# A two-stage attention and highway kernel: a fixed instruction order, a finer softmax chain, and part of the k norms taken off the matrix engine

## The chip, the cores and the metric

The kernel runs on one core of one Trainium2 chip. A core has five engines, each with its own in-order queue: TensorE (PE, with its weight loads shown as PEld), VectorE (DVE), ScalarE (ACT), GpSimd (POOL) and SyncE (SP, here used only to issue transfers). They meet through semaphores. The metric is the device time of one execution in microseconds. Before the change it was 270.34 us, the median of three runs (270.19 to 270.39). The profiled execution spans 268.3 us from its first to its last instruction; the difference of 2.0 us lies outside the span.

## What is computed

Four batches of q, k and v, each 6336 x 256 in float32, are turned into an attention over channels (a 256 x 256 matrix for each batch), and its result goes through a highway layer.

```python
qn = q / (np.linalg.norm(q, axis=1, keepdims=True) + 1e-06)     # norm over the 6336 rows
kn = k / (np.linalg.norm(k, axis=1, keepdims=True) + 1e-06)
s  = kn.transpose(0, 2, 1) @ qn / tau                           # 256 x 256 for each batch
a  = softmax(s, axis=-1)
x  = (v @ a).reshape(4 * 6336, 256)
H  = np.maximum(x @ w_h, 0.0)
T  = 1.0 / (1.0 + np.exp(-(x @ w_t + b_t)))
out = T * H + (1.0 - T) * x                                     # float32, 25344 x 256
```

The three inputs are 77.9 MB to read and the output is 26 MB to write.

## The kernel before

A batch has 50 row blocks s: 48 of 128 rows in 6 chunks of 8 (j = 0 to 5), and two of 96 rows (j = 6). Loads are issued by GpSimd and convert float32 to float16 on the way; stores and the four transposing transfers are issued by SyncE.

**Stage 1** of a batch multiplies k by q on TensorE for all 50 blocks, into two PSUM tiles. Beside the product itself it needs the sums of squares of each column of q and k. They are the diagonals of two more products, k by k and q by q:

```python
def stage1(b, s):                        # 50 of these for each batch
    for c in range(2):
        nc.tensor.matmul(sg[c][:, 0:C], kc, qa, ...)                  # 256 columns: the product
        nc.tensor.matmul(sg[c][:, C : C + P], kc, kc, ...)            # 128 columns: squares of k
        if not apart(b, s // CH):                                     # apart: b > 0 and j < 5
            nc.tensor.matmul(sg[c][:, C + P : C + 2 * P], qa[:, cs], qa[:, cs], ...)   # squares of q
```

For batches 1 to 3 the squares of the first five q chunks are made elsewhere: ScalarE squares half a chunk at a time (128 x 1024), GpSimd adds the halves and folds them, and one small matmul with a column of ones (`sumps`) sums over the partitions.

```python
nc.scalar.activation(out=sq, in_=qa, func=Act.Square)      # 30 of them
add(out=sq, in0=sq, in1=other)                             # GpSimd, 128x1024
add(out=sq[:, 0:2, :], in0=sq[:, 0:2, :], in1=sq[:, 2:4, :])      # 128x512
add(out=sq[:, 0, :], ...); add(out=sums[b], ...)           # 128x256 each
```

**The chain** between the stages turns the sums into softmax weights: `diagonal` reads the diagonals, `norm` is a power of 0.5 on GpSimd, `recip` and `dcat` make a diagonal matrix of the inverse norms, `bcast` spreads it with a matmul against ones, `scale` and `exp` make the softmax numerators, `trans` and `fold` multiply them by the two weight matrices, and `soft` and `evac_ah` write the three parts of the tiles `mr0` and `mr1`, which every matmul of stage 2 reads.

**Stage 2** of a batch takes 25 pairs of blocks; g counts them over all batches (0 to 99). For each pair: `tr` transposes v on TensorE and `ev` copies it out of PSUM (in the last batch chunks 3 to 6 are transposed by a transfer instead, four such transfers in all); `h`, `t` and `x` are four matmuls of 256 columns each; `b` sets the bias in PSUM by a copy; `r` (ReLU) and `g` (tanh) run on ScalarE; `p` and `y` on VectorE. A store takes four pairs.

```python
products(h, b, i, 1, ...)                       # h: 4 matmuls 128x256 on TensorE, line 800
copy(e, t[0:nr], bias_all[0:nr])                # b: ScalarE or VectorE
products(t, b, i, 2, ...)                       # t
nc.scalar.activation(out=d, in_=h, func=Act.Relu, scale=0.5)          # r
products(d, b, i, 0, ...)                       # x, added to d
nc.scalar.activation(out=uu, in_=t, func=Act.Tanh, scale=-0.5)        # g
nc.vector.scalar_tensor_tensor(out=pp, in0=uu, scalar=1.0, in1=d, ...)   # p
nc.vector.scalar_tensor_tensor(out=ot, in0=h, scalar=0.0, in1=pp, ...)   # y
```

The order of all of this on the engines is found while the program is built: each task has a key, and a small list scheduler (`Plan.run`, with the table of keys `PRIO`) picks what stands next. Loads stop between the end of stage 1 and the second norm (`loads_stop`). The tile buffers are 5 chunks for each of q, k and v and 7 for the output. Early stores are held back by small transfers (`hold`) that make SyncE wait for a later output chunk.

Of the kernel before, what the change touches and what calls it, by code (L numbers as in the profile page):

```python
# [15 lines left out]
P = 128  # L16
# [6 lines left out]
AHEAD = 16  # L23
BY_DMA = 3
SHORT = 1.08
MOVE = 165e3
APART = 5
V_AHEAD = 2


PRIO = {
    "tr": (24.974, 16.445, 34.195, 63.304),
    "ev": (74.59, 73.008, 67.512, 50.704),
    "h": (-53.39, -86.015, -64.208, -14.641),
    "bias": (-28.394, 23.065, -1.772, 4.453),
    "t": (4.111, -1.918, 67.766, 74.312),
    "relu": (46.555, -20.175, -1.498, 14.915),
    "x": (0.958, -19.433, 43.343, -6.4),
    "gate": (-54.132, 37.28, -94.231, -112.222),
    "prod": (-40.861, -10.819, -26.763, -55.482),  # L40
    "res": (53.604, 18.42, 116.457, -9.113),
    "s1": (117.419, 42.459, 84.45),
    "sq": (-15.195, 72.384, 19.395),
}
POW = 0.75
HEAD = 5.5
TAIL = 66
EV = BIAS = ("ACT", "DVE")
ENDS = [18, 48.5, 62.25]


class Ring:


    def __init__(self, bufs):
        self.bufs = bufs
        self.freed = []

    def open_at(self, t):
        n = len(self.freed) - self.bufs  # L60
        return n < 0 or (self.freed[n] is not None and self.freed[n] <= t)


class Task:
# [3 lines left out]

    def __init__(self, eng, key, pitch, lat, deps, fn, take=(), drop=(), size=0, follows=()):
        self.eng, self.key, self.pitch, self.lat = eng, key, pitch, lat
        self.deps, self.fn, self.take, self.drop, self.size = deps, fn, take, drop, size
        self.follows = follows
        self.start = self.done = None
        self.late = 0.0
        self.soft = 0
        self.held = {}
        self.serial = False

    def engines(self):
        return self.eng if isinstance(self.eng, tuple) else (self.eng,)

    def settle(self, e):
        n = self.eng.index(e)
        self.pitch, self.lat = self.pitch[n], self.lat[n]
        self.fn = partial(self.fn, e)
        self.eng = e


class Plan:

# [8 lines left out]
    def __init__(self):  # L101
        self.tasks = []
        self.rings = {}

        self.loads_stop, self.sums_stop = [], []

    def ring(self, tag, bufs):
        self.rings[tag] = Ring(bufs)

    def add(self, *args, **kw):  # L110
        t = Task(*args, **kw)
        self.tasks.append(t)
        return t

    def run(self):
        queues = {"POOL": [], "SP": []}
        in_order = {"POOL": [], "SP": []}
        users, followers = {}, {}
        for n, x in enumerate(self.tasks):
            x.n, x.left, x.at = n, len(x.deps) + len(x.follows), 0.0  # L120
            for d in x.deps:
                users.setdefault(d, []).append(x)
            for d in x.follows:
                followers.setdefault(d, []).append(x)
            if x.size or x.serial:
                in_order[x.eng].append(x)
        for lst in in_order.values():
            lst.sort(key=lambda x: (x.key, x.n), reverse=True)
        engines = list(dict.fromkeys(x.eng for x in self.tasks if not isinstance(x.eng, tuple)))
        avail = {e: [x for x in self.tasks if e in x.engines() and not x.left and not (x.size or x.serial)] for e in engines}  # L130
        free = dict.fromkeys(engines, 2.1)
        lanes, order, events = [], [], [0.0, 2.1]
        t, left = 0.0, len(self.tasks)
        eps = 1e-6

        def ready(x):
            return (
                not x.left
                and x.at <= t + eps
                and all(self.rings[g].open_at(t + eps) for g in x.take)  # L140
                and (x.eng != "POOL" or not x.size or sum(d > t + eps for d in lanes) < self.LANES)
            )

        def finish(x, when):
            x.done = when
            events.append(when)
            for owner, tag in x.drop:
                self.rings[tag].freed[owner.held[tag]] = when
            release(users.get(x, ()), when)

        def release(us, when):
            for u in us:
                u.left -= 1
                u.at = max(u.at, when)
                if not u.left and not (u.size or u.serial):
                    for e in u.engines():
                        avail[e].append(u)

        def pick(e):
            quiet = held(self.sums_stop)  # L160
            best = min(
                (x for x in avail[e] if ready(x) and not (quiet and x.soft >= quiet)),
                key=lambda x: (x.key, x.n), default=None,
            )
            lst = in_order.get(e)
            if best is None and lst and ready(lst[-1]) and not (e == "POOL" and held(self.loads_stop)):
                return lst[-1]
            return best

        def held(stops):  # L170
            return next(
                (
                    n + 1 for n, (a, b) in enumerate(stops)
                    if a.start is not None and (b.done is None or b.done > t + eps)
                ),
                0,
            )

        while left or any(queues.values()):
            for e in engines:  # L180
                x = pick(e) if free[e] <= t + eps else None
                if x is None:
                    continue
                if x.size or x.serial:
                    in_order[e].pop()
                else:
                    for other in x.engines():
                        avail[other].remove(x)
                    if isinstance(x.eng, tuple):
                        x.settle(e)  # L190
                left -= 1
                x.start = t
                order.append(x)
                for g in x.take:
                    x.held[g] = len(self.rings[g].freed)
                    self.rings[g].freed.append(None)
                free[e] = t + x.pitch
                release(followers.get(x, ()), free[e])
                events.append(max(free[e], t + 2 * eps))
                if x.size:  # L200
                    queues[e].append([x, float(x.size), t + self.HEAD])
                    events.append(t + self.HEAD)
                    if e == "POOL":
                        x.lane = len(lanes)
                        lanes.append(1e9)
                else:
                    finish(x, t + x.lat)

            act = [qq for qq in queues.values() if qq and qq[0][2] <= t + eps]
            share = self.RATE / max(1, len(act))  # L210
            nxt = [x for x in events if x > t + eps] + [t + qq[0][1] / share for qq in act]
            assert nxt, "no task can start"
            nxt = min(nxt)
            for qq in act:
                qq[0][1] -= share * (nxt - t)
            t = nxt
            events = [x for x in events if x > t - eps]
            for qq in act:
                if qq[0][1] < 1.0:
                    x = qq.pop(0)[0]  # L220
                    finish(x, t + self.LAG + x.late)
                    if x.eng == "POOL":
                        lanes[x.lane] = t + self.LAG
        self.end = max(x.done for x in order)
        return order
# [3 lines left out]
def kernel(  # L229
# [37 lines left out]
        "sq": 2, "vT": 3, "vT_t": 1, "o": O_BUFS, "ot": 1, "uu": 3, "pp": 3, "vtsb": 9, "mr0": 2, "mr1": 2,  # L267
        "sg0": 1, "sg1": 1, "vt": 1, "t": 1, "h": 2, "d": 2,
# [73 lines left out]
    def plan_load(nm, b, j, s=0, n=CH):  # L342

        size = P * n * C * 4 if j < NJ else TR * 2 * C * 4
        tag = nm if j < NJ else f"tail_{nm}"
        x = plan.add(
            "POOL", len(plan.tasks), 0.54, 0, [], lambda: load(nm, b, j, s, n),
            take=[tag] if s == 0 else [], size=size * (1 if j < NJ and n > 2 else SHORT),
        )
        ld.setdefault((nm, b, j), []).append(x)  # L350
        x.first = s
# [43 lines left out]
    plan_load("v", 0, 0)  # L395


    ends = [(-1, HEAD)] + [(e, (n + 1) * NS) for n, e in enumerate(ENDS)]

    def slot_of(n):  # L400

# [693 lines left out]
```

## Time and profile before

| what | value |
|---|---|
| time, median of 3 | 270.34 us |
| span of the profiled execution | 268.3 us |
| TensorE busy, idle | 246.4 us, 21.9 us |
| VectorE, ScalarE, GpSimd busy | 181.6, 195.1, 131.7 us |
| bytes read from and written to HBM | 78.38 MB, 25.95 MB |
| first matmul starts | 8.95 us |
| last stage-1 matmul of batch 0 starts | 36.69 us |
| first matmul of stage 2 (h of pair 0) | 45.65 us |
| first output store is issued | 101.04 us |
| last matmul starts | 262.04 us |
| last store is issued | 264.60 us |

In the lines of the profile a row names the line of the kernel, the engine, the operation and the tiles it writes and reads, then the number of instructions, the busy time in all and the mean of one in ns. Tables by window give the busy time of each engine in a stretch of the span. "GB/s" counts bytes as they land: a load reads four bytes of float32 from HBM for two bytes of float16 that land, so loads alone at 212 GB/s read 424 GB/s. A store counts once.

### The profile page before, as it was taken

What the parts mean: (1) busy time and instruction counts of PE and PEld (TensorE: products, weight loads), DVE (VectorE), ACT (ScalarE), POOL (GpSimd) and SP (SyncE); (2) the same over time, 40 slices, a digit from 0 to 9 for tenths busy, and PEclk for the clock granted to TensorE, in tenths of its full rate; (3) what the DMA queues carried; (4) which work ended last, traced back from release to release, by engine and by line L of the source; (5) the groups of instructions that cost most, each with busy time, mean ns of one, the idle gap of its engine ahead of it and who ended that gap; (6) DMA issues with size and microseconds to landing.
All of it is one profiled execution on the core that took longest, in us unless ns stands there. A gap on an engine that the chain in (4) does not pass through costs nothing.

```text
span 268.3 us, 6249 instructions
## 1 busy us (share of the span) xinstructions
PE 246.4 (92%) x2430; PEld 216.6 (81%) x2430; DVE 181.6 (68%) x377; ACT 195.1 (73%) x365; POOL 131.7 (49%) x167
## 2 busy tenths in 40 slices
PE   0697977999999999999999999999999999999991
PEld 0596864889989978999999878999998778888880
DVE  1000035777766789557878797586878998998994
ACT  1001016978888789999898887787798999998980
POOL 7233468688778064695689138567655110000000
PEclk9999999999999999999999999999999999999998
DMA  6999999999999999999999999999999999999995
GB/s 107 215 211 208 206 206 202 212 213 214 214 213 212 213 214 255 247 263 269 275 286 258 267 267 254 249 236 281 287 280 239 284 214 304 379 399 165 351 423 232
DMA packets 24622, 67.24 MB, mean 251 GB/s; under 512 B 9104, under 2 KB 11280, under 8 KB 21648
## 3 DMA queue, kind: packets, MB, share of 16 engines
q0 software_dynamic: 13472, 39.20, 75.0%
q1 hardware_dynamic: 11120, 27.64, 29.0%
q8 instruction: 19, 0.31, 0.4%
q14 instruction: 11, 0.09, 0.1%
HBM read 78.38 MB, written 25.95 MB: 389 GB/s over the span
## 4 chain that ended last, share of the span: by engine, by line
PE 76%; DMA 12%; ACT 5%; POOL 2%; issue 2%; DVE 2%; ACTq 0%; DVEq 0%; POOLq 0%
PE h L800 16%; PE t L800 16%; PE d L800 15%; PE sg L452 12%; DMA k<-in_k_dram 10%; PE sg L453 6%; PE vtps L760 5%; DMA v<-in_v_dram 2%; ACT uu L854 2%; PE sg L455 2%; PE t L831 1%; PE vtps L754 1%; PE ah L689 1%; POOL q L327 1%; ACT d L840 1%
## 5 line engine op out<-in xcount | busy, mean ns | idle before, releaser
L800 PEld LDWEIGHTS <-vtsb 128*128 128x128 f16 (+1 forms) x1044 | 98.8, 99 | 17.3 <-issue 3.2
L452 PE MATMUL sg<-q,k 128*128 128x256 f16 x384 | 83.8, 277 | 12.7 <-DMA k<-in_k_dram 12.6
L861 DVE SCALAR_TENSOR_TENSOR pp<-uu,d 128x512 f32<-128x512 f32 (+1 forms) x100 | 68.0, 684 | 28.4 <-PE d L800 16.1
L453 PE MATMUL sg<-k 128*128 128x128 f16 x384 | 76.8, 223 | 0.0
L854 ACT ACTIVATE uu<-t 128x512 f32<-128x512 f32 (+1 forms) x100 | 59.7, 597 | 19.1 <-PE t L800 18.5
L880 DVE SCALAR_TENSOR_TENSOR o<-h,pp 128x512 f32<-128x512 f32 x96 | 65.5, 686 | 1.7
L840 ACT ACTIVATE d<-h 128x512 f32<-128x512 f32 (+1 forms) x100 | 57.9, 584 | 5.7 <-PE h L800 4.9
L800 PE MATMUL t<-mr,vtsb 128*128 128x256 f16 (+1 forms) x348 | 52.2, 272 | 1.5 <-ACT t L533 1.2
L800 PE MATMUL h<-mr,vtsb 128*128 128x256 f16 (+1 forms) x348 | 51.2, 272 | 0.5 <-ACT vtsb L533 0.5
L800 PE MATMUL d<-mr,vtsb 128*128 128x256 f16 (+1 forms) x348 | 51.5, 272 | 0.1
L452 PEld LDWEIGHTS <-k 128*128 128x128 f16 x384 | 38.0, 99 | 16.7 <-DMA k<-in_k_dram 13.9
L476 POOL TENSOR_TENSOR sq<-sq,sq 128x1024 f32<-128x1024 f32 x15 | 35.4, 2361 | 16.7 <-ACT sq L470 16.6
L453 PEld LDWEIGHTS <-k 128*128 128x128 f16 x384 | 38.0, 99 | 1.5
L533 ACT COPY t<-bias_all 128x512 f32<-128x512 f32 (+1 forms) x60 | 35.4, 591 | 1.4
L455 PE MATMUL sg<-q 128*128 128x128 f16 x144 | 32.5, 226 | 0.0
L470 ACT ACTIVATE sq<-q 128x1024 f32<-128x1024 f16 x30 | 31.3, 1053 | 0.0
L760 PE MATMUL vtps<-ident,v 128*128 128x128 f32 x144 | 27.8, 275 | 0.9 <-DMA v<-in_v_dram 0.6
L569 DVE SCALAR_TENSOR_TENSOR junk<-sg,ident 128x128 f32<-128x128 f32 x16 | 4.6, 288 | 33.2 <-PE sg L455 32.7
L535 DVE COPY vtsb<-vtps 128x256 f32<-128x256 f32 (+2 forms) x47 | 19.6, 418 | 7.0 <-PE vtps L760 6.7
L327 POOL DMA_DIRECT2D v<-in_v_dram x24 | 13.7, 571 | 18.9 <-PE vtps L760 11.7
L327 POOL DMA_DIRECT2D q<-in_q_dram x28 | 15.4, 552 | 15.1 <-DMA q<-in_q_dram 7.1
L327 POOL DMA_DIRECT2D k<-in_k_dram x28 | 15.3, 548 | 13.1 <-DMA k<-in_k_dram 9.2
(78 smaller groups left out, 249.5 us busy)
## 6 DMA issues: line engine op xcount, KB each, us to landing
out_dram<-o SPq DMA_DIRECT2D x23, 1024.0 KB, 9.6
v<-in_v_dram POOLq DMA_DIRECT2D x24, 512.0 KB, 16.6
q<-in_q_dram POOLq DMA_DIRECT2D x21, 512.0 KB, 16.2
k<-in_k_dram POOLq DMA_DIRECT2D x21, 512.0 KB, 18.0
q<-in_q_dram POOLq DMA_DIRECT2D x5, 256.0 KB, 9.6
k<-in_k_dram POOLq DMA_DIRECT2D x5, 256.0 KB, 8.9
out_dram<-o SPq DMA_DIRECT2D x2, 512.0 KB, 4.2
out_dram<-ot SPq DMA_DIRECT2D x4, 192.0 KB, 5.1
```

Source lines behind the costliest of these rows:

```text
L327: nc.gpsimd.dma_start(out=t[:, s : s + n, :], in_=main_rows(src)[:, j * CH + s : j * CH + s + n, :])
L452: nc.tensor.matmul(sg[c][:, 0:C], kc, qa, start=first, stop=False)
L453: nc.tensor.matmul(sg[c][:, C : C + P], kc, kc, start=False, stop=False)
L455: nc.tensor.matmul(sg[c][:, C + P : C + 2 * P], qa[:, cs], qa[:, cs], start=False, stop=last)
L476: add(out=sq, in0=sq, in1=other)
L533: nc.scalar.copy(out=out, in_=in_)
L760: nc.tensor.transpose(ps[:, u, 0:nr], v.bitcast(f32), ident0[0:nr, 0:nr])
L800: nc.tensor.matmul(out[0:nr, u, :], vt[u][kt][:, 0:nr], mr[kt][:, col * C : (col + 1) * C], **flags(u, kt))
L840: nc.scalar.activation(out=d[0:nr, :, :], in_=ps_t["h", b, i][0:nr, :, :], func=Act.Relu, scale=0.5)
L854: nc.scalar.activation(out=uu[0:nr, :, :], in_=ps_t.pop(("t", b, i))[0:nr, :, :], func=Act.Tanh, scale=-0.5)
L861: nc.vector.scalar_tensor_tensor(out=pp[0:nr, :, :], in0=el.pop(("uu", b, i))[0:nr, :, :], scalar=1.0, in1=ps_t.pop(("d", b, i))[0:nr, :, ...
L880: nc.vector.scalar_tensor_tensor(out=ot, in0=ps_t.pop(("h", b, i))[0:nr, :, :], scalar=0.0, in1=el.pop(("pp", b, i))[0:nr, :, :], op0=AluO ...
```

## The change

1. **Order.** The scheduler and its keys are gone. Every task has a name, and one string, `ORDER`, lists all 1,528 of them as they are to be recorded, with the engine where there is a choice (`ev0/ACT`).
2. **Norms of k.** For batches 1 to 3, the squares of the first two k chunks leave TensorE, as those of five q chunks did already. The squares are made by ScalarE or VectorE, and a running sum is kept for each batch over all halves, by GpSimd or VectorE, with one fold at the end.
3. **A finer chain.** Diagonals, copies and evictions are separate tasks for each half; the diagonal matrix and the matmul against ones become two matmuls of an inverse norm, broadcast, against the identity; `evac_ah` is split into the part that `h` needs and the part that `t` needs, so that each product waits for its own part alone.
4. Buffers are given back in finer steps (for example `mr0` and `mr1` one by one).

Other forms of stage 2 that the new code can make (`form_b`, `form_d`) are not used: `FORM_B` and `FORM_D` are empty. The four transfers that transpose, the number of stores and loads and all tile sizes are as before.

```diff
-BY_DMA = 3
-APART = 5
-PRIO = { ... }
+BY_DMA = (3, 4, 5, 6)
+OFF = {'q': (0, 5, 5, 5), 'k': (0, 2, 2, 2)}
+ORDER = """
+Lq0.1 Lk0.0 Lq0.0 const Lk0.1 Lk0.2 Lq0.2 Lq0.6 Lk0.6 Lb0 Lb1 Lq0.3 s0.0 s0.1 ...
+... Lw1 s0.40 s0.41 Lv0.0 s0.42 s0.43 Lw0 s0.44 Lq1.0.4 s0.45 s0.46 s0.47 c0.dq1 c0.g0/ACT ball c0.dq0 c0.dk0
+c0.nq sqq1.0.0/ACT c0.dk1 c0.nk c0.iq c0.g1/ACT c0.b Lq1.1 c0.ik s1.0 s1.1 Lk1.1 s1.2 c0.s1 c0.s0 Lv0.1 ...
+"""
@@ stage1
-            nc.tensor.matmul(sg[c][:, C : C + P], kc, kc, start=False, stop=False)
-            if not apart(b, s // CH):
+            if not apart("k", b, s // CH):
+                nc.tensor.matmul(sg[c][:, C : C + P], kc, kc, start=False, stop=False)
+            if not apart("q", b, s // CH):
@@ squares and sums
-        nc.scalar.activation(out=sq, in_=qa, func=Act.Square)
+        if e == "ACT":
+            nc.scalar.activation(out=out, in_=x, func=Act.Square)
+        else:
+            (nc.vector if e == "DVE" else nc.gpsimd).tensor_tensor(out=out, in0=x, in1=x, op=AluOp.mult)
+    def add_square(nm, b, j, n, e):
+        eng, acc = nc.gpsimd if e == "POOL" else nc.vector, acc_t[nm, b]
+        eng.tensor_tensor(out=acc, in0=acc, in1=sq_t.pop((nm, b, j, n)), op=AluOp.add)
@@ chain
-            nc.tensor.matmul(st["cqb"], ones, st["dcat"][:, :, :], start=True, stop=True)
+            for c in range(2):
+                nc.tensor.matmul(
+                    st["cqb"][:, c, :], st["inv"][:, c : c + 1].to_broadcast([P, P]), ident0, ...)
-            o, a, r = mr_t[b][c][:, C : 3 * C], st["ah", c], st["ri"][:, c : c + 1]
+            o = rows_of(c)[:, (n + 1) * C : (n + 2) * C]
+            a, r = st["ah", c][:, n * C : (n + 1) * C], st["ri"][:, c : c + 1]
@@ stage 2
-                "PE", pr("h", g), 0.435, 0.64, [ev] + ready[b] + ends_of[h_bank], ...
+                f"h{g}", "PE", 0.437, 0.64, [ev] + ready[b]["h"] + ends_of[h_bank], ...
```

In `ORDER`, L is a load (Lv0.0 is v, batch 0, chunk 0), s a block of stage 1, c a step of the chain, sqk and adk a square and its addition, O a store, T a transposing transfer and H a hold.

## The prediction

> **What bounds the kernel now.** I read the page's first part, then its slices and queues. TensorE leads by far in busy time, and its slices stand at 9 almost from end to end. But so do those of the transfers:
>
> ```profile
> PE 246.4 (92%) x2430; PEld 216.6 (81%) x2430; DVE 181.6 (68%) x377; ACT 195.1 (73%) x365; POOL 131.7 (49%) x167
> ...
> PE   0697977999999999999999999999999999999991
> ...
> DMA  6999999999999999999999999999999999999995
> GB/s 107 215 211 208 206 206 202 212 213 214 214 213 212 213 214 255 247 263 269 275 286 258 267 267 254 249 236 281 287 280 239 284 214 304 379 399 165 351 423 232
> ...
> q0 software_dynamic: 13472, 39.20, 75.0%
> q1 hardware_dynamic: 11120, 27.64, 29.0%
> ...
> HBM read 78.38 MB, written 25.95 MB: 389 GB/s over the span
> ```
>
> Each slice is 6.7 us. The first 15 hold loads alone (the first store is issued at 101 us), and 212 GB/s landing means 424 GB/s read. Where loads and stores mix, the figure rises because a store counts once; the sum of bytes on the HBM side hardly changes. So the transfers run at one rate, about 424 GB/s, for nearly the whole span. Is TensorE held up by them? The table by window says where it idles, and the list of waits for whom:
>
> ```profile
> 38.00:46.00 8.00, 5.89 (x48) 4.10 (x49) 5.03 (x19) 4.30 (x10) 6.85 (x11) 1.00 1.14 199
> 46.00:100.00 54.00, 53.37 (x526) 47.21 (x524) 39.17 (x80) 46.09 (x84) 36.60 (x44) 1.00 1.07 213
> 100.00:200.00 100.00, 99.07 (x998) 89.54 (x997) 76.41 (x154) 85.82 (x156) 64.19 (x71) 1.00 1.06 264
> 200.00:262.00 62.00, 61.31 (x558) 52.27 (x556) 56.51 (x110) 56.25 (x113) 7.61 (x10) 1.00 1.05 308
> ```
>
> ```profile
> PE sg L452 <- DMA k<-in_k_dram: 12.6, 5, 9.0
> ...
> PE t L800 <- ACT t L533: 1.2, 3, 0.7
> ...
> PE vtps L760 <- DMA v<-in_v_dram: 0.6, 1, 0.6
> ```
>
> The second column after the window is TensorE's busy time. From 46 to 262 us it idles 216.0 - 53.37 - 99.07 - 61.31 = 2.25 us. Before 46 it waits for k, above all 9.0 us for the first chunk, and 2.1 us are idle between 38 and 46, in the chain of batch 0. So TensorE bounds the stretch from 46 on, and its work there is back to back. Yet the transfers have a floor of their own that lies close under the same span. I work it out:
>
> - Start: the first two loads, 2.10 MB read, have landed at 8.95 us when TensorE starts; at 424 GB/s they take 4.95 us, so bytes flow from 4.0 us.
> - Bytes: (78.38 + 25.95) MB / 424 GB/s = 246.1 us.
> - The transposing transfers. The second queue carried 27.64 MB against 25.95 MB stored, so 1.69 MB of transposes: three full chunks and a quarter. The transfer view of 240 to 262 us shows what they cost:
>
> ```profile
> GB/s 387 298 188 61 45 39 142 290 324 247 161 140 45 236 254 188 500 447 268 462 256 358 86 462 462 268 477 477 447 477 268 462 477 462 447 283 477 432 447 417
> ```
>
> Here a slot is 0.55 us. From the second to the sixteenth, 8.25 us, only 2658 x 0.55 = 1.46 MB land; two full transposes (1.04 MB) lie there, and the other 0.42 MB would take 1.0 us. So one costs (8.25 - 1.0) / 2 = 3.6 us, and 3.25 of them 11.8 us. The last 17 slots, stores alone, average 426 GB/s.
> - Sum: 4.0 + 246.1 + 11.8 = 261.9 us, and some 1.5 us (my estimate) from the last byte to the end: **263.4 us** against a span of 268.3. The slack of the transfers is 4.9 us, under 2%.
>
> [...] shares of 75.0% and 29.0% add to over 100% and say nothing, the bytes do. [...] the 684 ns of line 861 at 512 and the 414 ns of line 634 at 256 lead, by their slope of 1.05 ns, to 1.22 us as well. [...]
>
> **The change part by part.**
>
> *Squares of k.* 3 batches x 2 chunks x 8 blocks x 2 halves = 96 matmuls of 128 columns leave TensorE. Their own length in the trace (220 ns) is latency; what counts is the distance to the next start:
>
> ```profile
> 38.33 0.28 PE L452 MATMUL sg<-q,k 128*128 128x256 f16 x1 [1.43 <-DMA k<-in_k_dram]
> 38.45 0.22 PE L453 MATMUL sg<-k 128*128 128x128 f16 x1
> 38.51 0.27 PE L452 MATMUL sg<-q,k 128*128 128x256 f16 x1
> 38.62 0.22 PE L453 MATMUL sg<-k 128*128 128x128 f16 x1
> ```
>
> From 38.45 to 38.51: 0.056 us, so 96 x 0.056 = 5.4 us less. What comes back: three sums over partitions for k, of the kind of line 516, 0.50 us each in the chain view, 1.5 us; and the new broadcast of the inverse norms, four short matmuls for two long ones, some 0.1 us a batch. **Net on TensorE: -3.5 us**, all of it after 38 us, where TensorE is the bound.
>
> *Squares and sums elsewhere.* From the lists of both instruction orders: ScalarE makes 28 squares for 30 (-2 x 1.05), 17 more copies of transposed v (about +6.3), 4 fewer of the wide ones (-2.4), 2 more bias copies (+1.2), and small ones: about +4 us, to 199. VectorE makes 14 squares and 5 sums at 1.22 (+23.2), folds (+1), 17 fewer copies of 0.42 (-7.1) and 4 more of the wide ones (+1.7), 2 fewer bias copies (-1.4), no diagonal matrices (-1.9): about +15 us, to 197. GpSimd makes 31 sums of 2.36 us and 9 us of folds for 74.4 us before: about +8 us, to 140. All three stay near or under three quarters of the span, beside TensorE and not on its path.
>
> *Chain.* In batches 1 to 3 it was nearly hidden: all idle time of TensorE there is within the 2.25 us. In batch 0 the first h starts at 45.65 us after v's first chunk, issued only at 38.88 us. The new order issues that load before block 42 of stage 1, and the parts of the chain overlap more. I put the first pair about 1.5 us earlier. But fewer matmuls of stage 1 are left to fill the gap, as k's squares are gone there, so TensorE gains at most 1.5 us from it.
>
> *Order.* The tasks are mostly where they were: stage 1 of batch 1 ends near pair 18, of batch 2 near pair 43, of batch 3 near pair 64, before and after. I give it nothing of its own. Stage 1 of batch 0 waits for its loads in both.
>
> Sum for TensorE alone: -3.5 - 1.5 = -5.0 us.
>
> **Rivals.** First, *the gain passes through*: 270.3 - 5.0 = 265.3 us. For it speaks that TensorE is without gaps from 46 to 262. Second, *the transfers become the bound*: the bytes and the transposes are unchanged, so at best the span loses 4.9 us, and that only with no gap anywhere. For it speaks that the final stores already run at the full rate from 251 us to the end, behind stores queued at 220 us and transposes; pairs done earlier then only wait in the output buffers. Against it, some of the slack (the dip to 199 GB/s between 38 and 46) goes away with the earlier load of v. I expect 266.5 to 268 us. Third, *VectorE and GpSimd collide*: 19 long operations on VectorE meet GpSimd sums that run a third of the time; waits of up to 2.4 us each in fixed queues could stall TensorE, whose d and h have two PSUM buffers each. That would give 269 to 274 us. The 70 us that VectorE would still be idle speak against it.
>
> **How the number follows.** I take the second as the likeliest: of 5.0 us won on TensorE and 4.9 us of slack in the transfers some 3.1 us come through. 270.3 - 3.1 = **267.2 us**. The range runs from the first rival, 265.3, to a small loss by the third that eats most of the gain, 269.7. Faster by over 2% means under 264.9 us, a span of 262.9, below the floor I worked out: 6%. Slower by over 2% needs stalls of over 8 us net: 4%.
>
> **What would show it.** Right: 288 matmuls of the k-by-k form and TensorE busy time near 243; loads still at 212 GB/s in the first 14 slices; stores at full rate to the end; TensorE with new idle time, or its last matmul earlier by more than the span shrinks, so that the last store ends several us after it. The first h near 44 us. Wrong: a span under 263, which would mean that the transposes cost less beside other traffic than I counted or that the rate can rise; or GpSimd sums well over 2.36 us and VectorE sums well over 1.22 us, with TensorE waiting for d, t or h, which would be the collision.

## The result, and the profile after

The changed kernel takes **307.54 us** (median of four, 306.54 to 308.66) beside 270.26 us for the kernel before: a ratio of 1.138, 95% interval 1.133 to 1.143. It is 37 us slower; 267.2 was predicted, and 269.7 was the upper end of the range.

The page of the changed kernel, the same parts and rows as were shown of before (a slice is now 7.7 us):

```profile
PE 254.4 (83%) x2354; PEld 218.1 (71%) x2354; DVE 209.0 (68%) x383; ACT 200.6 (65%) x385; POOL 140.6 (46%) x150
...
PE   0599877888899999899978896799996999563793
...
DMA  6999999999997999999999999949799999998997
GB/s 122 214 211 207 205 212 214 209 182 198 214 211 138 212 210 201 361 217 199 174 269 212 245 196 276 270 79 405 139 192 352 389 66 104 252 58 193 337 335 285
...
q0 software_dynamic: 13472, 39.20, 69.4%
q1 hardware_dynamic: 11120, 27.64, 31.3%
...
HBM read 78.38 MB, written 25.95 MB: 340 GB/s over the span
```

The bytes are the same to the last digit, and so is most of the work. But the row of 9s is broken: TensorE stands at 5, 6, 3 and 7 near the end, and the transfers fall to 138, 79, 139, 66, 104 and 58 GB/s in single slices; before, only the first slice and one late one (165) lay under 200. Near the end the DMA row stands at 9 in slices where only 66, 104 and 58 GB/s land, so its share does not tell the rate here. The table by window says where TensorE's idle time lies (the second column after the window is its busy time):

```profile
38.00:46.00 8.00, 5.47 (x24) 3.42 (x25) 6.64 (x20) 4.37 (x12) 6.73 (x10) 0.79 1.15 211
46.00:100.00 54.00, 48.04 (x449) 41.23 (x449) 47.75 (x67) 40.90 (x76) 34.81 (x32) 0.97 1.02 195
100.00:200.00 100.00, 89.52 (x808) 77.47 (x806) 79.59 (x153) 79.40 (x153) 66.28 (x60) 0.97 1.03 234
200.00:262.00 62.00, 59.28 (x575) 52.05 (x574) 49.98 (x102) 53.22 (x107) 15.74 (x15) 1.00 0.97 218
262.00:307.00 45.00, 26.55 (x202) 20.96 (x200) 23.70 (x37) 20.65 (x39) 0.53 (x1) 0.84 1.00 241
```

Before, TensorE idled 0.6 us from 46 to 100 and 0.9 from 100 to 200; now 6.0 and 10.5, and some 18 after 262. Between 38 and 46 it runs 24 matmuls where it ran 48. The list of waits of the changed kernel has three that were absent before, or short (engine and line that waited, for what, us in all, times, longest):

```profile
PE h L731 <- DVE o L864: 21.8, 7, 6.6
POOL v L262 <- DMA vT<-v: 21.0, 1, 21.0
DVE o L864 <- DMA out_dram<-o: 20.3, 4, 7.0
```

Read from the bottom: VectorE cannot write a result because its output buffer is still being stored; the next h needs the PSUM buffer that this result would free; and GpSimd cannot issue a load of v because its buffer is still being transposed. A wait for an output buffer was not on the list of before at all, and GpSimd's wait for a transpose was 2.2 us there.

How far the kernel has come is told by the start of the last VectorE operation of a pair (line 880 before, 864 after), in us:

| pair | before | after | e1 | e3 | e9 |
|---|---|---|---|---|---|
| 0 | 48.4 | 51.5 | 52.4 | 49.6 | 48.5 |
| 20 | 99.6 | 108.2 | 107.1 | 103.7 | 100.5 |
| 44 | 159.2 | 173.7 | 169.0 | 169.9 | 160.4 |
| 64 | 205.7 | 226.7 | 216.7 | 223.1 | 208.1 |
| 80 | 236.6 | 258.6 | 245.8 | 254.7 | 239.2 |
| 88 | 248.4 | 286.2 | 258.0 | 277.7 | 250.9 |
| 99 | 263.9 | 302.8 | 273.1 | 294.8 | 266.4 |

The loss grows in steps: 3 us in the first chain, 15 by pair 44, 22 by pair 80, 39 at the end. It has more than one cause.

### The profile page after: what moved, and what is told of

Same layout as the page of the kernel before. It is cut to its first block, busy times and chain, and to the rows that moved or that the text cites. A ratio compares the mean times of both kernels' runs of the same rounds, so it can differ in the third digit from the quotient of the medians.

```text
span 306.7 us, 6113 instructions
## 1 busy us (share of the span) xinstructions
PE 254.4 (83%) x2354; PEld 218.1 (71%) x2354; DVE 209.0 (68%) x383; ACT 200.6 (65%) x385; POOL 140.6 (46%) x150
## 4 chain that ended last, share of the span: by engine, by line
PE 40%; DMA 33%; DVE 15%; issue 4%; SPq 3%; ACT 2%; POOL 2%; DVEq 0%; ACTq 0%; POOLq 0%
DMA out_dram<-o 13%; PE h L731 8%; PE sg L373 8%; PE t L731 8%; PE d L731 7%; DMA v<-in_v_dram 7%; DMA q<-in_q_dram 5%; DMA out_dram<-ot 5%; DVE pp L818 4%; DMA k<-in_k_dram 4%; PE vtps L691 4%; DVE o L864 4%; PE sg L375 3%; SPq L699 2%; DVE sq_k L400 1%
## 5 line engine op out<-in xcount | busy, mean ns | idle before, releaser
L731 PEld LDWEIGHTS <-vtsb 128*128 128x128 f16 (+1 forms) x1044 | 101.6, 100 | 41.3 <-issue 26.6
L373 PE MATMUL sg<-q,k 128*128 128x256 f16 x384 | 81.9, 280 | 12.4 <-DMA q<-in_q_dram 11.4
L404 POOL TENSOR_TENSOR acc_q<-acc_q,sq_q 128x1024 f32<-128x1024 f32 x24 | 57.6, 2401 | 44.7 <-ACT sq_q L398 25.5
L731 PE MATMUL h<-mr,vtsb 128*128 128x256 f16 (+1 forms) x348 | 53.9, 279 | 20.0 <-DVE o L864 15.2
L375 PE MATMUL sg<-k 128*128 128x128 f16 x288 | 60.0, 224 | 0.0
L373 PEld LDWEIGHTS <-k 128*128 128x128 f16 x384 | 38.7, 101 | 13.2 <-DMA k<-in_k_dram 9.9
L375 PEld LDWEIGHTS <-k 128*128 128x128 f16 x288 | 28.7, 100 | 3.7 <-issue 2.4
L482 ACT COPY gs<-sg 128x256 f32<-128x256 f32 x8 | 3.0, 377 | 35.2 <-PE sg L377 35.2
L482 ACT COPY vtsb<-vtps 128x256 f32<-128x256 f32 (+2 forms) x53 | 20.4, 385 | 5.4 <-PE vtps L691 5.2
L731 PEld LDWEIGHTS <-vT 128*128 128x128 f16 x144 | 15.1, 105 | 10.7 <-issue 7.6
L691 PEld LDWEIGHTS vtps<-ident,v 128*128 128x128 f32 x144 | 17.1, 145 | 4.5 <-ACT et L482 1.1
```

Source lines behind the costliest of these rows:

```text
L373: nc.tensor.matmul(sg[c][:, 0:C], kc, qa, start=first, stop=False)
L375: nc.tensor.matmul(sg[c][:, C : C + P], kc, kc, start=False, stop=False)
L404: eng.tensor_tensor(out=acc, in0=acc, in1=sq_t.pop((nm, b, j, n)), op=AluOp.add)
L482: nc.scalar.copy(out=out, in_=in_)
L691: nc.tensor.transpose(ps[:, u, 0:nr], v.bitcast(f32), ident0[0:nr, 0:nr])
L731: nc.tensor.matmul(out[0:nr, u, :], vt[u][kt][:, 0:nr], mr[kt][:, col * C : (col + 1) * C], **flags(u, kt))
```

## The experiments

| run | what it is | us | against before beside it |
|---|---|---|---|
| e1 | SyncE's order of before | 279.29 | 270.04, single runs |
| e2 | next batch's squares and sums after each chain | 316.90 | 270.04, single runs |
| e3 | all squares on ScalarE | 300.57 | 270.04, single runs |
| e4 | no load beside a transpose | 292.44 | 270.04, single runs |
| e5 | e1 and e3 | 280.61 | 1.039 (1.033 to 1.045) |
| e6 | e5, k's squares back on TensorE | 279.38 | 1.032 (1.028 to 1.037) |
| e7 | e5, holds one chunk later | 291.83 | 1.080 (1.074 to 1.085) |
| e8 | e5, end of SyncE's order from the change | 288.33 | 1.068 (1.061 to 1.075) |
| e9 | order of before on all engines, k on TensorE | 273.12 | 1.009 (1.004 to 1.014) |
| e10 | e9, k's squares apart | 286.97 | 1.061 (1.055 to 1.067) |
| e11 | e9, sums moved | 273.50 | 1.013 (1.011 to 1.015) |
| e12 | e11, k's squares apart, clear of the chains | 284.44 | 1.053 (1.051 to 1.055) |
| e13 | e12, 24 bias copies to VectorE | 283.77 | 1.047 (1.042 to 1.053) |
| e14 | k's squares on VectorE | 293.12 | 1.084 (1.079 to 1.089) |
| e15 | e11, matmuls left out, nothing in their place | 275.36 | 1.015 (1.010 to 1.021) |
| e16 | e11, twelve squares added, nothing taken away | 278.93 | 1.028 (1.024 to 1.033) |

All of them use the code of the changed kernel and change its `ORDER`, and little else.

### One cause at a time: e1 to e4

Three theories stood after the two traces were compared. **S**: SyncE's order of stores and holds. In the kernel before, each hold makes a store wait until the output is five chunks ahead; in the new order it is mostly six, and there are seven output buffers. Near the end three stores (O2.2, O2.3 and O3.1) stand behind transposing transfers and behind stores of later chunks. **C**: the collision of VectorE and GpSimd. The kernel before holds GpSimd's sums back during each chain; the new order does not. The timeline of the changed kernel, in its first chain (start, us, engine, line):

```profile
44.13 2.77 DVE L599 TENSOR_SCALAR mr<-e,ri 128x256 f16<-128x256 f32 x2
44.38 2.36 POOL L404 TENSOR_TENSOR acc_k<-acc_k,sq_k 128x1024 f32<-128x1024 f32 x1
```

Two small evictions, 0.35 us each before, take 2.77 us together, the second 2.5 us, and end just after GpSimd's sum. **T**: transposes beside loads. Here are the transposes' time from issue to landing (median) before and after, GpSimd's issues of the last two loads of v in the changed kernel, and then its timeline from 262 us on:

```profile
vT<-v SPq DMA_TRANSPOSE x3, 6.1
```

```profile
vT<-v SPq DMA_TRANSPOSE x3, 19.2
```

```profile
241.44 0.53 POOL L262 DMA_DIRECT2D v<-in_v_dram  x1 [11.84 <-PE vtps L691]
262.97 0.53 POOL L262 DMA_DIRECT2D v<-in_v_dram  x1 [21.00 <-DMA vT<-v]
```

```profile
262.25 5.96 SPq L699 DMA_TRANSPOSE vT<-v  x1
...
270.52 0.69 DVE L864 SCALAR_TENSOR_TENSOR o<-h,pp 128x512 f32<-128x512 f32 x1 [6.56 <-DMA out_dram<-o]
271.26 1.01 PE L731 MATMUL h<-mr,vtsb 128*128 128x256 f16 x4 [6.46 <-DVE o L864]
```

These medians must be read with care, because a landing includes the wait behind stores issued earlier: one by one, the three full transposes landed in 5.0, 20.8 and 6.1 us before, and in 22.2, 19.2 and 4.3 after. The packets tell more. A full transpose moves 2,048 packets of 256 bytes, and the transfer records of the two traces have them here (first to last start, us):

| transpose | before | changed kernel |
|---|---|---|
| first | 216.6 to 219.8 | 244.2 to 261.5 |
| second | 240.6 to 245.2 | 265.0 to 279.3 |
| third | 245.7 to 249.1 | 283.8 to 286.4 |

So the slow landing of before (20.8 us) was a wait behind other transfers, of which 362 GB/s landed from 221 to 240 us. In the changed kernel each of the last two loads of v is issued within 1.3 us of a transpose (240.21 and 262.25); the packets of these two transposes take 17.3 and 14.3 us for 3 to 5 before, the stores wait with them, and the wait for an output buffer runs through VectorE to TensorE.

**e1**, the stores, holds and transposes in SyncE's order of before, nothing else:

```diff
-H6 O0.0 H5 O0.1 O0.2 H9 O0.3 ... O2.4 T3.3 O2.5 O2.2 T3.4 O2.3 T3.5 O3.0 H7 O3.2 ...
+H5 O0.0 O0.6 H6 O0.1 H7 O0.2 H8 O0.3 ... O1.5 T3.3 H17 O2.0 ... O2.5 T3.4 O2.6 T3.5 O3.0 T3.6 O3.1 ...
```

> The changed kernel with one thing put back: SyncE's queue (holds, stores, transposing transfers) stands in the order of the kernel before, where the store of chunk n waits for the first result of chunk n+5, one store for each hold; in the changed order it mostly waits for n+6, some stores stand behind later ones, and the last four stand behind the transposes. Theory S (stores issued too late for seven output buffers): VectorE's waits for stores to land, 20.3 + 4.7 us in the changed kernel, go to under 5 us, and the time falls from 307.5 to about 280 to 285 us. Theory C (GpSimd sums block VectorE): under 3 us are won, above 304 us. Theory T (a transpose that runs beside a load crawls, and what stands behind it in the queue waits): falls only if the transposes happen to lie free of loads again, then their part, some 14 us, is in the gain as well.

279.29 us. The waits for output buffers are gone, and 28 of the 37 us are back. The order of 46 transfer issues on an engine that computes nothing was the largest cause. T is part of this gain: with the stores in order the transposes lay free of most of the load traffic, and their packets took 3.2 to 3.5 us.

**e2**, GpSimd's sums and the squares of the next batch moved behind each chain in `ORDER`:

```diff
-c0.nq sqq1.0.0/ACT ... sqk1.0.0/DVE c0.e0 ... sqk1.0.1/DVE ... c0.a0 adk1.0.1/POOL c0.a1 ...
+c0.nq ... c0.e0 ... c0.a0 c0.a1 sqq1.0.0/ACT sqk1.0.0/DVE sqk1.0.1/DVE adk1.0.1/POOL ...
```

> The changed kernel with the squares and sums of the next batch moved from inside each softmax chain to just behind it; the kernel before held its sums back there, the changed order does not. Theory C: the two copies of the softmax rows in the chain of batch 0, 2.77 us together in the changed kernel, take 0.7 us again, the first stage-2 results start 2 us earlier, and the whole wins 3 to 6 us: 302 to 304 us. Theory S: the start of each batch wins and the later waits for stores give it back: 306 to 308 us.

316.9 us, slower still. The evictions were back at 0.33 to 0.35 us, and the pairs of batch 0 came 1.1 to 1.6 us earlier than in the changed kernel. The loss starts at the second chain: from pair 22 to pair 26 the run falls back by 10 us, as the squares and sums of k now came late and TensorE's queue stood at the sum over partitions (8.9 us there):

```profile
PE sumps_k L418 <- POOL sums_k L407: 15.2, 2, 8.9
```

**e3**, the fourteen squares on VectorE made by ScalarE (`sq.../DVE` to `sq.../ACT`):

> The changed kernel with its 14 VectorE squares on ScalarE. Theory C: the VectorE squares have two SBUF inputs and took 1.75 us on the mean against 1.22 us undisturbed; without them VectorE has 24 us less to do, GpSimd sums no longer meet them, and the time falls by 3 to 6 us. Theory S: within 2 us of 307.5.

300.57 us: 1.9 us won at pair 0, where the evictions were back at 342 ns, and 7 us in all. VectorE's 16.2 us of waits for output buffers remained. C is real, and small; an inverse-norm step in the third chain still took 2.2 us for 0.16, so this run does not remove all of it.

**e4**, seven v buffers for five, and the last two loads of v issued early:

```diff
-V_BUFS = 5
+V_BUFS = 7
-... Lv3.2 ... Lv3.4 ... Lv3.5 ...
+... Lv3.2 Lv3.4 Lv3.5 ...
```

> The changed kernel with seven v buffers for five, and the last two v loads of batch 3 issued 5 to 10 pairs earlier, so that they have landed when the transposing transfers run. Theory T: each full transpose takes about 4 us again, where two of them took 12 to 17 us beside a load, the stores behind them in the queue land earlier, and 10 to 17 us of the tail go: 290 to 298 us. Theories S (hold and order of stores alone) and C: within 3 us of 307.5.

292.44 us: 15 us won, all of it after pair 80. Transposes landed in 10.3 us (median), and the packets of each full one, with no load beside them, took 2.9 to 3.5 us. T is real, and most of the loss near the end.

### What in SyncE's order costs: e5 to e8

**e5** joins e1 and e3.

> Both cures at once: SyncE's order of before, and all squares on ScalarE. If the loss has two separate causes, the order of stores with its waits, and VectorE held up beside GpSimd's sums in the chain of batch 0, both gains are kept: the store order gave 28 us, and the squares moved the first pairs 2.9 us earlier. Expected 271 to 276 us, chain 0 at +1 us against before, and nothing like line L864's waits for out_dram. If the squares' gain of 7 us was a by-product of the disturbed stores, it stays at 279. If the change brought its 3.5 us less TensorE work through, under 270.

280.61 us: no better than e1. (Pair 0 had come 1.9 us earlier in e3, not the 2.9 us of the expectation.) The 7 us of e3 were won only against the disturbed stores; with the stores in order the 1.7 us won at pair 0 are gone by pair 52 (190.0 us for 189.6 in e1). The causes do not add.

**e6** puts k's squares back on TensorE (`OFF` for k is 0 in every batch, and their tasks leave `ORDER`).

> The run before this one, with the squares of k back on TensorE: 96 more short matmuls, 5.4 us by their distances, less 1.6 us for sums over partitions. If TensorE bounds this version, it is 3 to 4 us slower than the other. If what bounds is the transfers, or what ScalarE and GpSimd do for the squares, the same within 1 us, or faster.

279.38 us, not 3 to 4 us slower. Putting 96 matmuls back and taking the squares and sums of k away nets to nothing that can be told from e5, as the intervals meet. With the sums the long waits in the chains went too: the inverse-norm steps took up to 2.2 us in e5 and 0.15 to 0.19 us here. So what the matmuls alone cost is not shown by this run.

**e7** moves the holds of e5 by one chunk:

```diff
-H5 O0.0 O0.6 H6 O0.1 H7 O0.2 ... H15 O1.4 H16 O1.5
+H5 H6 O0.0 O0.6 H7 O0.1 H8 O0.2 ... H16 O1.4 O1.5
```

> As the run with both cures, but the stores of chunks 0 to 10 each wait for one output chunk more (seven buffers, six chunks ahead, as in most of the changed kernel's order); the end of the order as before. If VectorE's waits for output buffers come from these holds, the run is 5 to 10 us slower than with both cures, with waits of DVE on out_dram in the middle, from 150 to 230 us. If the loss comes from the end of the order alone, it is the same within 1 us.

291.83 us, 11 us slower than e5, and its list of waits has the row back:

```profile
DVE o L859 <- DMA out_dram<-o: 9.7, 5, 4.0
```

With seven buffers, one chunk more of holding leaves no buffer free while a store of 1 MB is on its way.

**e8** takes e5 and the end of the change's order:

```diff
-O1.5 T3.3 H17 O2.0 O2.1 O2.2 O2.3 O2.4 O2.5 T3.4 O2.6 T3.5 O3.0 T3.6 O3.1 O3.2 O3.3 O3.4
+O1.5 O2.0 O2.1 O2.4 T3.3 O2.5 O2.2 T3.4 O2.3 T3.5 O3.0 O3.2 O3.3 T3.6 O3.1 O2.6 O3.4 H17
```

> As the run with both cures, but from the third batch's stores on SyncE's order is that of the change: the first transposing transfer stands beside the load of v's fifth chunk, and three stores stand behind transposes. If stores behind transposes and transposes beside loads make most of the 28 us, this is 12 to 20 us slower than with both cures, with transposes of 10 us and more and VectorE waiting for out_dram. If it is the holds in the middle, under 3 us slower.

288.33 us, 7.7 us slower than e5 and less than expected. One transpose ran beside a load again: its packets took 15.4 us, those of the other two full ones 2.5 and 2.9.

Holds (11.2) and end (7.7) make 18.9 us together; e3 against e5, the whole of SyncE's order with the same squares, makes 20.0. The two parts thus make up nearly all of what SyncE's order costs, with T inside the second.

### The other engines' order: e9 to e11

**e9** writes the whole order of before, engine by engine, as an `ORDER`, without k's squares. What stays of the change is the finer chain and the running sums.

```diff
-c0.dq1 c0.g0/ACT ball c0.dq0 c0.dk0 ... s1.0 s1.1 s1.2 ... s1.3 ... tr0 ... t0 ... s1.4 h0 ...
+c0.dq0 c0.dq1 c0.dk0 ... s1.0 s1.1 s1.2 s1.3 s1.4 s1.5 s1.6 s1.7 ... tr0 ... h0 t0 r0 ...
-OFF = {'q': (0, 5, 5, 5), 'k': (0, 2, 2, 2)}
+OFF = {'q': (0, 5, 5, 5), 'k': (0, 0, 0, 0)}
```

> The changed kernel's code with ORDER written to be the order of the kernel before, engine by engine (loads, pairs, blocks of stage 1, squares on ScalarE, stores and holds), and without the squares of k: what stays of the change is the finer chain and the running sums. What is left open after the first runs is a loss of 9 us with the stores' order of before, of which TensorE idles 1 to 2 us in nearly every stretch of 20 us. If the order of the pairs on the engines makes it, this comes back to 269 to 271 us, and TensorE has no idle time from 46 to 262. If it is the new code (split chain, two more small copies, f32 running sums), it stays at 276 to 280.

273.12 us, between the two expectations. e6 does nearly the same work with the same order of stores, and takes 6 us more: the order of pairs, blocks and loads, and the choice of engine, which differs for 113 tasks (mostly copies of transposed v and of the bias). Two lines of the table by window, e6 first, show the largest single place:

```profile
38.00:46.00 8.00, 6.16 (x31) 3.92 (x32) 3.04 (x16) 4.14 (x11) 5.58 (x10) 0.65 1.15 212
46.00:60.00 14.00, 13.18 (x123) 11.12 (x122) 9.17 (x15) 9.94 (x20) 3.93 (x4) 0.96 1.07 213
```

```profile
38.00:46.00 8.00, 5.77 (x48) 4.13 (x49) 4.96 (x19) 4.44 (x10) 6.84 (x11) 1.00 1.15 197
46.00:60.00 14.00, 13.28 (x124) 11.24 (x122) 9.09 (x15) 11.48 (x21) 8.73 (x9) 1.00 1.06 213
```

e9 fits eight blocks of the next batch's stage 1 between the steps of the chain, e6 four before its first t: 48 matmuls against 31, these on a TensorE granted 0.65 of its clock. Pair 0's h starts at 45.8 us in e9 and 48.1 in e6.

**e10** is e9 with k's squares apart again, on ScalarE beside q's.

> The run before this one, with the squares of two k chunks a batch taken off TensorE as in the change: 12 more squares on ScalarE (1.05 us each), 9 more sums of 2.36 us and folds on GpSimd, 96 short matmuls less. By the prediction's second rival 266.5 to 268 us (TensorE 3.5 us less, the transfers' floor at 265.4). If ScalarE, 73% busy, has no room where the squares stand, 270 to 274 us.

286.97 us: 14 us slower than e9, far above both expectations. **e11** puts the last two sums of each batch next to each other on GpSimd, and the last sum over partitions a step later.

> The order of before in the new code once more, without the squares of k, with the last chunk's two sums of each batch next to each other on GpSimd and the last batch's sum over partitions one step later on TensorE. In the run without this TensorE's order had the sum over partitions ahead of a GpSimd sum that had moved 2.4 us later. If the 2.7 us that were left come from that, 270 to 271.5 us; if from the finer chain's extra instructions, 272.5 to 273.5.

273.50 us: no gain. By the starts of pairs, e11 loses 1.0 us by pair 64, 1.2 in the last chain and 1.3 after the last pair. In the last chain TensorE waits for GpSimd's last sum (0.9 us, with no such row in the list of before):

```profile
PE sumps_q L415 <- POOL sums_q L404: 0.9, 1, 0.9
```

That wait was not removed in any run, and the rest of the 2.4 to 3.5 us that e9 and e11 lack stays open.

### Where the squares of k cost: e12 to e16

**e12** takes e11 and places k's squares and sums by hand behind each chain, with more buffers:

```diff
-OFF = {'q': (0, 5, 5, 5), 'k': (0, 0, 0, 0)}
-BUFS = {}
+OFF = {'q': (0, 5, 5, 5), 'k': (0, 2, 2, 2)}
+BUFS = {"k": 6, "sq": 4}
+... sqk1.0.0/ACT r4 ... sqk1.0.1/ACT g4 ... adk1.0.1/POOL ... sqk1.1.0/ACT g7 ... sqk1.1.1/ACT r8 ...
```

> The run beside it, with the squares of two k chunks a batch apart, but placed by hand clear of the four chains: squares on ScalarE and sums on GpSimd only after the chain's last eviction, four square buffers for two, six k buffers for five, so that no load waits for a square. If part 2 is worth what its matmuls are worth (96 x 0.056 us less 1.5 us), and only its place was wrong, 266.5 to 268.5 us, faster than both kernels. If ScalarE has no room for 12 more squares of 1.05 us, or the transfers are the floor, 270 to 273.

284.44 us: both expectations fell. Matched task by task with e11, TensorE falls behind by 0.5 to 1 us at most of the squares, by 2.5 us in the third chain (a sum on GpSimd still ran into it), and at sums over partitions, as here in its timeline:

```profile
88.56 0.72 POOL L407 TENSOR_TENSOR sums_q<-acc_q 128x256 f32<-128x256 f32 x1
...
89.34 0.61 PE L418 MATMUL sumps_q<-ones,sums_q 128*128 128x1 f32 x4 [1.09 <-POOL sums_q L407]
```

GpSimd had k's sums to make as well (19.9 of 20 us busy from 60 to 80, 15.6 in e11), so q's came late, and TensorE's queue stood.

**e13** gives ScalarE its time back (24 `b.../ACT` to `b.../DVE` near the squares, later sums); **e14** makes the squares on VectorE (`sqk.../DVE`) with the biases left on ScalarE.

> As the run with k's squares on ScalarE clear of the chains, but for each of the twelve squares the next two bias copies go to VectorE (24 x 0.60 us off ScalarE, 24 x 0.69 us onto VectorE), the first sums after a chain on GpSimd stand some 2 us later, and the first batch's sum over partitions too. If the squares cost what they hold ScalarE up, most of the 11 us come back: 268 to 274 us. If it is GpSimd's sums and the sums over partitions that TensorE waits for, 279 to 284.

> The same with the twelve squares on VectorE (1.22 us each alone) and no bias copy moved. VectorE is 65% busy and ScalarE 73%. If VectorE has room, 269 to 274 us. If a square on VectorE waits for GpSimd's sums (1.75 us in the mean in the changed kernel) and holds the products behind it, 275 to 282 us.

e13: 283.77 us, as e12, though ScalarE is busy 194.8 us for 206.4; TensorE now waits for VectorE's copies of the bias (3.2 us). So relieving ScalarE alone does not help. e14: 293.12 us, far above both expectations. The groups of its VectorE squares (count, busy, mean ns):

```profile
L395 DVE TENSOR_TENSOR sq_k<-k 128x1024 f32<-128x1024 f16 x9 | 17.9, 1989 | 0.0
...
L395 DVE TENSOR_TENSOR acc_k<-k 128x1024 f32<-128x1024 f16 x3 | 5.4, 1795 | 0.0
```

In the changed kernel the nine squares on VectorE that met no sum on GpSimd took 1.21 to 1.22 us each, and four of the five that met one 2.2 to 3.8; these here took 2.0 and 1.8 in the mean.

**e15** leaves the 96 k-by-k matmuls out and makes the squares nowhere, so its norms of k lack those rows; **e16** leaves all matmuls and adds twelve squares of constants to ScalarE's queue, where e12 has its own, into a tile that nothing reads.

```diff
-            if not apart("k", b, s // CH):
+            if not (b > 0 and s // CH < 2):
```

```diff
             assert all(id(d) in done for d in [*x.deps, *x.follows]), name
+            for _ in range(EXTRA.get(name, 0)):
+                self.extra()          # ScalarE: spare = Square(wht), 128x1024
```

> The order of before in the new code, with the 96 k-by-k matmuls of two chunks a batch left out and nothing in their place, so that the norms of k are those of the other rows only. By the prediction 96 x 0.056 = 5.4 us less on TensorE. If TensorE bounds and nothing lies close under it, 268 us. If the transfers' floor of 265.4 holds part of it back, 269 to 271. If the relief brings nothing, because TensorE then waits in the same places, 273.

> The order of before in the new code with nothing taken off TensorE, and twelve squares of the same shape (128x1024, read from the constant weights, written to a tile that nothing reads) put into ScalarE's queue where the run with k apart on ScalarE had its twelve. If a square in the queue costs TensorE most of its length, 12 x 1.05 = 12.6 us at most: 280 to 286 us. If ScalarE has room beside TensorE, 273 to 275; the 11 us then come from the sums on GpSimd and over partitions.

e15: 275.36 us, no gain. The interval of its ratio (1.010 to 1.021) lies wholly above 0.993, where 5.4 us less than e11 would be. Before the third chain TensorE comes only 0.6 us ahead of e11, for 3.6 us of matmuls left out by then; then a sum on GpSimd runs into that chain, in its timeline:

```profile
162.75 2.83 DVE L591 TENSOR_SCALAR mr<-e,ri 128x256 f16<-128x256 f32 x1
163.05 2.36 POOL L396 TENSOR_TENSOR acc_q<-acc_q,sq_q 128x1024 f32<-128x1024 f32 x1
...
166.42 0.61 PE L723 MATMUL h<-mr,vtsb 128*128 128x256 f16 x4 [2.48 <-DVE mr L631]
```

The collision costs 2.5 us, and the last pair comes 1.6 us later than in e11. Without it, as an estimate from these two numbers, e15 would have gained some 1 us of the 5.4. TensorE's waits for loads hardly grow (14.7 us in all, e11 14.5), which speaks against the transfers as what held it back.

e16: 278.93 us, between its expectations. Its rows of waits (1.4 and 0.3 us in e11):

```profile
PE t L728 <- ACT t L479: 4.3, 8, 0.9
...
PE d L728 <- ACT d L785: 1.2, 3, 0.5
```

By the ratios (each 0.01 is 2.7 us) the squares alone cost 4.2 us, give or take 1.3, a third of their 12.6; in the traces the last pair comes 6.0 us later than in e11. The relief alone costs 0.7, within its uncertainty; both with the sums (e12) cost 10.7 (10.2 at the last pair). The remaining 4 to 6 us belong to the sums and to what the parts do to each other; that was not split further.

No version here beats the kernel before.

## Why the prediction was wrong

**The step that failed first is "Order. ... I give it nothing of its own."** It compared where stage 1 of each batch ends among the pairs, found the same places, and stopped. The order of before with k's squares still apart takes 21 to 23 of the 37 us away (e10, e12); with k's squares back on TensorE as well it is 34 (e9). Going step by step from the changed kernel, the squares taken off VectorE gave 7 us (e3), SyncE's holds, stores and transposes 20 (e5), k's squares put back 1, which can't be told from zero (e6), and the pairs, blocks, loads and choices of engine 6 (e9). These shares depend on the path: SyncE's order taken first gave 28 (e1), and k's squares cost 14 and 11 us in the order of before (e10, e12). What was wrong can be seen in the two orders, though not what it costs: holds six chunks ahead for seven buffers, stores out of turn behind transposes, loads issued next to transposes, and nothing that kept GpSimd's sums out of the chains.

**The second step that failed, "Net on TensorE: -3.5 us", was right as a count and wrong as time.** The changed kernel has the 288 k-by-k matmuls, though TensorE is busy for 254.4 us in it, not near 243 (its granted clock was 0.954 over the run, 0.997 before). But the 5.4 us of matmuls left out bring nothing in the order of before even by themselves (e15), and with squares and sums elsewhere in their place the move cost 11 to 14 us (e12, e10). "TensorE bounds the stretch from 46 on, and its work there is back to back" was true of the trace; that work taken away shortens it did not follow. With one piece out, TensorE waited more for other engines: 2.4 us for ScalarE's bias copies ahead of t (1.4 in e11), and 2.5 us in the third chain.

**"All three stay near or under three quarters of the span, beside TensorE and not on its path."** The loads came out as worked out for ScalarE (200.6 for 199) and GpSimd (140.6 for 140); VectorE has 209.0 for 197, as its ten squares of q took 1.75 us each for 1.22 (the prediction's estimate for 1024 elements) and the small operations of the chains waited too. The conclusion was wrong: twelve squares on ScalarE, 73% busy, cost about 4 us of time (e16). A share over the span did not tell how long one instruction waits in its queue.

**Chain.** "I put the first pair about 1.5 us earlier", first h near 44 us: it starts at 48.6, 3 us later than before. "Fewer matmuls of stage 1 are left to fill the gap" was the right thought, and the new order filled even less of it. With the order of before the finer chain starts h at 45.8 and 45.5 us (e9, e11), for 45.65 before: it gains nothing that these runs show.

**The transfers' floor** was right about bytes and assumed no gap. It counted 3.6 us for each transpose everywhere. That fits the 3 to 5 us of packets before; beside a load it was 14 and 17. Its 1.5 us from the last byte to the end, an estimate, fit the 1.6 of before's records (the last store packet ends at 266.8 us, the span at 268.3). Of the cost beside other traffic the prediction had said only that it might be less. Rival 2 named the right resource, as a floor under a gain and not as a loss.

**The third rival**, VectorE against GpSimd, was right in kind: small operations waited for whole sums, and TensorE for them. Its 269 to 274 us were too small for the result because it is the smallest of the causes found: 1.9 us at pair 0, and nothing that shows in the time once the stores are in order (e1, e5). Its waits of up to 2.4 us were an estimate, the length of one GpSimd sum (2.36 us); the trace of before shows no such wait. It counted the long operations alone. Here operations with one tensor operand were held up as well, one 128x256 eviction of eight (0.35 us to 2.5) and the 128x2 one of the inverse norms (0.16 to 0.56 in the mean). Why they are held up, no trace here says.

## What to carry to other kernels

An order found by a scheduler can hold policies, such as how far stores are held back or what stays out of a chain; when it is rewritten by hand, look for each of them in the new order, on the queue that only issues transfers too. A full TensorE queue in a tuned kernel does not mean that work taken from it comes back as time: leave the work out altogether and measure that first, before building its replacement. Judge a neighbour engine by the queue at the place where the new work lands, not by its share of the span.

## What the runs showed of the hardware

The packets of a full transposing transfer (0.5 MB) took 2 to 5 us with hardly any load under way (3.2 to 4.6 before, 2.9 to 3.5 in e4) and 12 to 17 us beside a load that converts to float16 (17.3 and 14.3 in the changed kernel, 16.0 and 11.8 in e3, 15.4 in e8). In the changed kernel the core moved 66, 104 and 58 GB/s in three of the four slices from 245 to 276 us, behind the transposes issued at 240 and 262 us. Time from issue to landing is no measure of it: one transpose of before needed 20.8 us to land and 4.6 us for its packets. A VectorE operation of 128x256 elements took 2.8 us, for 0.35 elsewhere, when a sum on GpSimd started 0.3 us after it (e15); it ended 0.2 us after the sum. The granted TensorE clock from 38 to 46 us was 0.65 in e6 (31 matmuls there) and 0.79 in the changed kernel (24), but 1.00 in e12 (34) and in e9 and before (48 each). It was 0.84 from 262 us on in the changed kernel; in before's tables it was 1.00 up to 262 and 0.88 from there (4 matmuls). Whether the low clock was a cause of any loss was not tried.
